# Block 1's attention in 32-token chunks, q rows issued by POOL, memory rows of v loaded once per batch

## The chip, the cores and the metric

The kernel runs on one core of one Trainium2 chip. Times are device microseconds of one execution; a comparison uses the median of several executions. The engines are TensorE (PE, with its weight loads as PEld), VectorE (DVE), ScalarE (ACT), GpSimd (POOL) and SyncE (SP). DMAs are issued from SP's queue, which the profile calls hardware_dynamic, and from POOL's, software_dynamic.

## The reference

Chunked attention with memory rows, then two feed-forward layers with different gates. In float32:

```python
# q, k, v: (4, 8, 768, 64); mem_k, mem_v: (4, 8, 8, 64); chunk 32, 16 keys to the left, 8 to the right
for c in range(768 // 32):
    l_start, r_end = max(0, 32*c - 16), min(768, 32*c + 32 + 8)
    k_full = concat([mem_k, k[:, :, l_start:r_end]]); v_full = concat([mem_v, v[:, :, l_start:r_end]])
    a = softmax(q_c @ k_full.T / 8)
    out[:, :, chunk c] = a @ v_full
x = out as (3072 tokens, 512)
h = x @ moe_w_in; x = (h * tanh(softplus(h))) @ moe_w_out       # 512 -> 2048 -> 512
h = x @ moe2_w_in; x = (h * sigmoid(1.702 * h)) @ moe2_w_out
```

The weights come as float64 and are turned into float32 on the chip.

## The kernel before

**Tiling and stages.** The 3072 tokens are cut into 8 blocks of 384 (TB), two to a batch. `quads` makes the attention of one block after the other, `forward` the first product of layer 1 (16 column tiles f of w_in, 128 columns each). Block 0's `forward` takes float32 matmuls (4 per f, each recorded as two instructions); from block 1 on weights and inputs are split into a high and a low part and three products are summed (12 per f). In the page's lines `forward` is L1218. After block 7's `forward` come the other three products (`across`, `first`, `second`), which the change doesn't touch.

**Two forms of attention.** The rows form (`rows_of_heads`, `turned`, `quad`) serves blocks 0 and 1. It loads rows of q, k and v with 64 channels (256 bytes) of all heads for two groups of 96 queries at a time, 120 keys and 8 memory rows to a group; PE turns q and k (L761), the copies out of PSUM are L768 (ACT) or L769 (DVE); scores are L829 in block 0 and L789 in block 1; VectorE masks and takes the row extremes (L845), ScalarE takes the exponentials (L860), VectorE normalises (L880); PE turns the result (L911 or L991) and multiplies it with v (L928 or L1013). Block 0 goes by `quad_out`, block 1 by `oct_scores` and `oct_out`, which do four groups in one go. The chunk form (`pair_of_heads`, `values_of`, `duo`) serves blocks 2 to 7. It works on 32 queries against 64 keys (16 + 32 + 8 and 8 memory keys). q and k come in pieces of 32 channels (128 bytes) and are turned by VectorE (L669, L672); the memory keys are turned once per batch (`memory_keys`, L632) and copied behind each chunk's keys (L676). A `duo` covers two pairs of heads, so a block has two: scores L1054, VectorE's extremes L1069, exponentials L1076, normalisation L1088, PE's turn L1096, values L1116, then the two parts of x (L1128 or L1130, and L1132).

**Loads.** Rows of blocks 0 and 1, q and k of the later ones, and all weights are issued by SP, one queue in order; block 0's rows may be issued by POOL too (`early`), whichever the planner finds free sooner. v of blocks 2 to 7 is issued by POOL (`via`), 6 loads to a `values_of` (per pair of heads two runs of v and one of mem_v), 12 to a duo.

**Order.** Every step is an `add` with a rank, the engines it may run on with an assumed cost, and what it reads and writes. `Plan.issue` simulates the engines with these costs and hands out, at each moment, the ready step of lowest rank on each engine; that order is the program's order on that engine, and nothing is reordered on the chip. A load is ready when its buffer is free; its assumed transfer time is `bus(bytes, run)`. Ranks count column tiles: `forward(j, f)` has rank 16 j + f. Block 0's attention starts at rank -20, block 1's at -4, block j's at 16 (j-1) - 12 from block 2 on; the loads stand 4 to 8 ahead. The w_in tiles of layer 1 are loaded at rank f - 4.5 (`w_first`), turned into float32 at f - 1.5 (L416 or L419, L425, L429, L433) and split at f + 6 (`w_cut`, L529, L534).

**Buffers.** `T` holds named buffers. In block 0 and 1 the chunk buffers don't exist; at block 2 `more` takes five weight buffers (wo11 to wo15) and `Spread` lays q, k, their turned forms and v (`vh`, four places, two to a duo) over them, z0, z1, z3 and two more `vt`.

Of the kernel before, what the change touches and what calls it, by code (L numbers as in the profile page):

```python
# [9 lines left out]
F32 = mybir.dt.float32  # L10
# [8 lines left out]
EARLY = 2  # L19
WARM = 16  # L20
LEAD = 8
# [5 lines left out]
STAGGER = 1.5  # L27
# [272 lines left out]
def bus(nbytes, run):  # L300
    return nbytes / 290e3 * (1 if run >= 512 else 1.3 if run >= 256 else 1.8)
# [3 lines left out]
def kernel(  # L305
# [64 lines left out]
    def load(rank, buf, parts, nbytes, run, reads=(), early=False, via=None):  # L370

        for part in parts:
            def go(queue, part=part):
                o, i = part()
                queue.dma_start(out=o, in_=i)  # L375

            size = bus(nbytes / len(parts), run)
            ways = [
                ("sp", 0.475, lambda go=go: go(nc.sync), size),
                ("pool", 1.2, lambda go=go: go(nc.gpsimd), size),  # L380
            ]
            add(rank, [("pool", 0.8, *ways[1][2:])] if via else ways if early else ways[:1], reads=reads, writes=[buf])
# [254 lines left out]
    def pair_of_heads(j, hp, rank):  # L637
# [29 lines left out]
        load(rank - 4, ql, qs, P * TB * 4, 128)  # L667
# [20 lines left out]
    def values_of(j, h0, rank):  # L688
# [4 lines left out]
        for i in range(2):  # L693
# [8 lines left out]
            for row, n, r0, c, many in runs:  # L702
# [28 lines left out]
    def rows_of_heads(j, gp, rank):  # L731

        b, s0 = divmod(j * TB, S)
        n = NF - 4 + 2 * j + gp
        qs, ks, vt = (T[nm].new([P, 2, H, D], F32) for nm in (f"wi{n}", f"wo{n}", "vt"))
# [11 lines left out]
        load(rank - 4, ks, kp, size, 256, early=j == 0)  # L747
        load(rank - 4, qs, qp, size * GQ // P, 256, early=j == 0)
        load(rank - 2, vt, vp, size, 256, early=j == 0)
        return qs, ks, vt  # L750

    def turned(j, hp, gp, st, rank):
        qs, ks, _ = st
        t = T["h"].new([P, 2 * (GQ + P)], F32)
        name = ("kT", "qT")[(gp if j else hp) % 2] if j == 0 or hp % 2 else "u"
# [21 lines left out]
    def oct_scores(pairs, rank, names):  # L777

        reads, writes = [x for pair in pairs for p in pair for x in p[2]], []
        cost = 1.4 + 1.0 * (len(pairs) - 1)  # L780
        out = [[T[n].new([GQ, GB, P], F32) for n in ns] for ns in names]

        def scores():
            for pair, s in zip(pairs, out):
                for queries, keys, _ in pair:
                    for i in range(2):
# [24 lines left out]
    def quad(j, hp, gp, heads, rank, given=None, both=None):  # L811
# [64 lines left out]
        if not both:  # L876
            inverses(rank, sm, r)
# [845 lines left out]
```

## Time and profile before

| | us |
|---|---|
| median of 3 runs | 1104.11 |
| lowest and highest run | 1103.93, 1105.63 |
| the profiled execution | 1105.13 |
| its span, first to last instruction | 1103.3 |
| PE, DVE, ACT, POOL busy | 1079.3, 800.3, 555.8, 98.6 |

The profile is of one execution. Busy shares are averages over stages with different limits, so the page is read together with the busy times by stage, the timelines of single engines and the list of waits. A wait is put down to what came last. The ends of matmuls are modelled; the step from one start to the next is the safer measure of what a matmul takes.

### The profile page before, as it was taken

To read this page: it belongs to the slowest core of one execution; us is meant where nothing else is said; L and a number is where in the kernel's file an instruction comes from. 1 tells how busy PE (TensorE), PEld (TensorE's weight loads), DVE (VectorE), ACT (ScalarE), POOL (GpSimd) and SP (SyncE) were. 2 spreads that over 40 slices of the span, in tenths; PEclk is the share of its full clock that TensorE was granted. 3 is DMA by queue.
4 is the path that set the end of the run, shared out by engine and by line. 5 is a ranking of instruction groups with operands and counts; after the bars stand their busy time and mean duration, and the time that the engine had idled before them with its cause. 6 is when DMAs were issued, how large, how long until landed. Compare 5 with 4: busy or idle time off the path is not lost.

```text
span 1103.3 us, 24808 instructions
## 1 busy us (share of the span) xinstructions
PE 1079.3 (98%) x9642; PEld 1041.1 (94%) x9642; DVE 800.3 (73%) x1456; ACT 555.8 (50%) x1246; POOL 98.6 (9%) x169
## 2 busy tenths in 40 slices
PE   7899999999999999999999999999999999999998
PEld 6568898989999999999999999999999999999998
DVE  5997656756556688899879856666657787877875
ACT  5875453545454455555455565555555533333332
POOL 2005642432300000000000000000000000000000
PEclk9999999999999999999999999999999999999999
DMA  9988998899986854663552686868688536345361
GB/s 172 264 241 189 242 247 228 205 250 268 278 276 222 249 175 147 216 212 121 189 172 86 208 260 223 296 227 290 203 265 261 160 106 166 112 133 145 105 165 46
DMA packets 278733, 221.28 MB, mean 201 GB/s; under 512 B 113553, under 2 KB 253868, under 8 KB 278616
## 3 DMA queue, kind: packets, MB, share of 16 engines
q1 hardware_dynamic: 272055, 209.46, 64.9%
q0 software_dynamic: 6560, 10.24, 3.8%
q8 instruction: 76, 1.25, 0.5%
q14 instruction: 42, 0.34, 0.1%
HBM read 138.33 MB, written 81.26 MB: 199 GB/s over the span
## 4 chain that ended last, share of the span: by engine, by line
PE 78%; DMA 10%; DVE 5%; SPq 4%; issue 1%; ACT 1%; DVEq 0%; ACTq 0%
PE o L1481 9%; PE o L1573 9%; PE h L1218 9%; PE o L1218 8%; PE h L1380 7%; PE o L1380 6%; PE s L1481 6%; PE h L1573 6%; PE h L1481 6%; PE s L1573 5%; SPq L375 4%; PE s L1380 3%; DMA st<-wd 3%; DMA st<-in_moe_w_out_dram 2%; DMA g1d<-ev 1%
## 5 line engine op out<-in xcount | busy, mean ns | idle before, releaser
L1218 PE MATMUL h<-xh,wi 128*128 128x384 f32 x320 | 82.9, 340 | 0.0
L1218 PE MATMUL o<-xh,wi 128*128 128x384 f32 x320 | 82.7, 339 | 0.0
L1218 PEld LDWEIGHTS h<-xh,wi 128*128 128x128 f32 x320 | 57.2, 188 | 0.6
L1218 PEld LDWEIGHTS o<-xh,wi 128*128 128x128 f32 x320 | 57.0, 188 | 0.5
L1218 PE MATMUL h<-xl,wi 128*128 128x384 f32 x160 | 53.7, 336 | 0.0
L1218 PE MATMUL o<-xl,wi 128*128 128x384 f32 x160 | 53.7, 336 | 0.0
L1350 ACT ACTIVATE e<-h 128x384 f32<-128x384 f32 (+2 forms) x47 | 22.4, 477 | 45.4 <-PE h L1573 28.8
L1573 PE MATMUL o<-wo,xh 128*128 128x256 f32 x232 | 43.7, 282 | 0.0
L1563 DVE TENSOR_TENSOR xl<-vt,xh 128x1024 fp32r<-128x1024 f32 x24 | 29.3, 1223 | 19.7 <-ACT xh L1560 18.0
L1563 DVE TENSOR_TENSOR xl<-wi,xh 128x1024 fp32r<-128x1024 f32 x32 | 38.8, 1222 | 5.9 <-ACT xh L1560 5.1
L1481 PE MATMUL o<-xh,wo 128*128 128x256 f32 x224 | 40.5, 282 | 0.0
L1560 ACT ACTIVATE xh<-wi 128x1024 fp32r<-128x1024 f32 x25 | 26.4, 1056 | 23.0 <-DMA wi<-gd 12.4
L375 POOL DMA_DIRECT2D vt<-in_v_dram x50 | 32.2, 648 | 63.3 <-PE o L1116 33.6
L375 POOL DMA_DIRECT2D wo<-in_v_dram x50 | 31.7, 638 | 53.7 <-PE o L1116 51.1
L1464 DVE TENSOR_TENSOR xl<-z,xh 128x1024 fp32r<-128x1024 f32 x24 | 29.2, 1222 | 9.7 <-ACT xh L1460 9.1
L1218 PE MATMUL o<-wo,wi 128*128 128x384 f32 x192 | 36.2, 340 | 0.0
L1573 PEld LDWEIGHTS o<-wo,xh 128*128 128x128 f32 x232 | 36.0, 190 | 0.0
L1218 PE MATMUL h<-wo,wi 128*128 128x384 f32 x192 | 35.7, 339 | 0.0
L1481 PEld LDWEIGHTS o<-xh,wo 128*128 128x128 f32 x224 | 34.6, 190 | 0.0
L1218 PEld LDWEIGHTS h<-wo,wi 128*128 128x128 f32 x192 | 33.2, 188 | 0.2
L1218 PEld LDWEIGHTS o<-wo,wi 128*128 128x128 f32 x192 | 33.0, 188 | 0.4
L1350 ACT ACTIVATE ev<-o 128x384 f32<-128x384 f32 (+2 forms) x31 | 14.5, 469 | 36.7 <-PE o L1573 17.5
(460 smaller groups left out, 3499.6 us busy)
## 6 DMA issues: line engine op xcount, KB each, us to landing
st<-in_moe_w_out_dram SPq DMA_DIRECT2D x32, 512.0 KB
st<-wd SPq DMA_DIRECT2D x29, 512.0 KB
z<-g1d SPq DMA_DIRECT2D x24, 512.0 KB
vt<-gd SPq DMA_DIRECT2D x24, 512.0 KB
wi<-gd SPq DMA_DIRECT2D x24, 512.0 KB
g1d<-gl SPq DMA_DIRECT2D x46, 192.0 KB
g1d<-z SPq DMA_DIRECT2D x45, 192.0 KB
wi<-in_moe_w_in_dram SPq DMA_DIRECT2D x16, 512.0 KB
```

The source lines that it names most:

```text
L375: queue.dma_start(out=o, in_=i)
L1218: nc.tensor.matmul(out=h.get(), lhsT=a[:, c], rhs=b.at(kk), start=(n == 0), stop=(n == KD * len(prods) - 1))
L1350: ("act", act(n, True), lambda: nc.scalar.activation(out=dst(), in_=bank.get(), func=AF.Copy)),
L1380: nc.tensor.matmul(out=bank.get(), lhsT=a, rhs=b, start=(fresh and m == 0), stop=(m == 3 * K2 - 1), skip_group_check=not fresh,)
L1464: add(rank + 0.05, [("dve", dve(n2), lambda gh=gh, gl=gl, src=src: nc.vector.tensor_tensor(out=flat(gl), in0=flat(src), in1=flat(gh), op=A ...
L1481: nc.tensor.matmul(out=bank[:, d, :], lhsT=a, rhs=b[:, p, :], start=(fresh and h == d == p == m == 0), stop=(h == 1 and p == HP - 1 and m ...
L1560: ("act", act(NP * P), lambda: nc.scalar.activation(out=flat(gh), in_=flat(src), func=AF.Copy)),
L1563: add(rank + 0.05, [("dve", dve(NP * P), lambda: nc.vector.tensor_tensor(out=flat(gl), in0=flat(src), in1=flat(gh), op=ALU.subtract))], re ...
L1573: nc.tensor.matmul(out=bank.get(), lhsT=a[:, p], rhs=b, start=(fresh and p == 0 and m == 0), stop=(p == NP - 1 and m == 2), skip_group_che ...
```

## The change

Block 1 goes through the chunk form (`pair_of_heads`, `values_of`, `duo`) instead of the rows form. `EARLY`, `LEAD`, `STAGGER`, `oct_scores`, `oct_out` and the arguments that served them go. The chunk buffers are laid out at block 1, in another order of places: the first duo's q, k and v go to wo11 to wo15 and only later ones to z0, z1 and the two `vt`. Block 0's staging buffers move from wo12 and wo13 to wo8 and wo9. `memory_keys` is called for the first batch too, at rank -9. q from block 2 on is issued by POOL (`via=NARROW * (j > 1)`); a load from POOL has an assumed cost of 0.64 instead of 0.8. `values_of` loads the memory rows of v only in the first block of a batch and in block 1; in blocks 3, 5 and 7 the four `vh` places still hold them. `bus` assumes other transfer times: longer ones for short rows from SP, shorter ones from POOL. All of block j + 1's attention is handed to the planner before `forward(j, 0)`, in block 1 too.

```diff
-EARLY = 2
-LEAD = 8
-STAGGER = 1.5
+NARROW = 0.64
...
-def bus(nbytes, run):
-    return nbytes / 290e3 * (1 if run >= 512 else 1.3 if run >= 256 else 1.8)
+def bus(nbytes, run, soft=False):
+    if soft:
+        return nbytes / 290e3 * (1.07 if run >= 256 else 1.45)
+    return nbytes / 290e3 * (1 if run >= 512 else 1.75 if run >= 256 else 1.93)
...
-    def load(rank, buf, parts, nbytes, run, reads=(), early=False, via=None):
+    def load(rank, buf, parts, nbytes, run, reads=(), via=0, either=False):
...
-            size = bus(nbytes / len(parts), run)
-            ways = [
-                ("sp", 0.475, lambda go=go: go(nc.sync), size),
-                ("pool", 1.2, lambda go=go: go(nc.gpsimd), size),
-            ]
-            add(rank, [("pool", 0.8, *ways[1][2:])] if via else ways if early else ways[:1], reads=reads, writes=[buf])
+            way = ("sp", 0.475, lambda go=go: go(nc.sync), bus(nbytes / len(parts), run))
+            if via:
+                way = ("pool", via, lambda go=go: go(nc.gpsimd), bus(nbytes / len(parts), run, True))
+            ways = [way]
+            if either:
+                ways.append(("pool", 1.2, lambda go=go: go(nc.gpsimd), bus(nbytes / len(parts), run, True)))
+            add(rank, ways, reads=reads, writes=[buf])
...
-        load(rank - 4, ql, qs, P * TB * 4, 128)
+        load(rank - 4, ql, qs, P * TB * 4, 128, via=NARROW * (j > 1))
...
-            parts.append(lambda row=i * D + CHUNK, h=h: (
-                vt[row:row + NM], rows(mem_v, h * NM, [(1, NM), (0, NCH)], 0, D)
-            ))
-        load(rank, vt, parts, P * NCH * D * 4, 256, via="pool")
+            if s0 == 0 or j == 1:
+                parts.append(lambda row=i * D + CHUNK, h=h: (
+                    vt[row:row + NM], rows(mem_v, h * NM, [(1, NM), (0, NCH)], 0, D)
+                ))
+        load(rank, vt, parts, P * NCH * D * 4, 256, via=NARROW)
...
-        n = NF - 4 + 2 * j + gp
-        qs, ks, vt = (T[nm].new([P, 2, H, D], F32) for nm in (f"wi{n}", f"wo{n}", "vt"))
+        n = NF - 4 + gp
+        qs, ks, vt = (T[nm].new([P, 2, H, D], F32) for nm in (f"wi{n}", f"wo{n - 4}", "vt"))
...
-    def oct_scores(pairs, rank, names):
...
-    def oct_out(j, rank, vt, heads):
...
-            if j == EARLY:
+            if j == 1:
...
-                T["ql"] = Spread(pre, (z0, 0), (more[3], 0))
-                T["kl"] = Spread(pre, (z0, TB), (more[3], TB))
-                T["qT"] = Spread(pre, *((z, 0) for z in (z1, *more[:2])))
-                T["kT"] = Spread(pre, *((z, 448) for z in (z1, *more[:2])))
+                T["ql"] = Spread(pre, (more[3], 0), (z0, 0))
+                T["kl"] = Spread(pre, (more[3], TB), (z0, TB))
+                T["qT"] = Spread(pre, *((z, 0) for z in (*more[:2], z1)))
+                T["kT"] = Spread(pre, *((z, 448) for z in (*more[:2], z1)))
...
-                T["vh"] = Spread(pre, *((z, 0) for z in (*vs, more[2], more[4])))
+                T["vh"] = Spread(pre, *((z, 0) for z in (more[2], more[4], *vs)))
...
-            base = NF * (j - 1) - (4 if j < EARLY else SOON)
-            if s0 == 0 and j + 1 >= EARLY:
-                memory_keys(b, base)
+            base = NF * (j - 1) - (4 if j < 2 else SOON)
+            if s0 == 0:
+                memory_keys(b, base + (11 if j == 0 else 0))
...
-                attention(j + 1, (f + LEAD) // 2 if j + 1 < EARLY else NQ)
+                attention(j + 1, NQ)
```

## Rows read from the trace of the kernel before

**Rows 1.** The page: busy time, the chain that ended last, POOL's queue.
```profile
PE 1079.3 (98%) x9642; PEld 1041.1 (94%) x9642; DVE 800.3 (73%) x1456; ACT 555.8 (50%) x1246; POOL 98.6 (9%) x169
...
q0 software_dynamic: 6560, 10.24, 3.8%
...
PE 78%; DMA 10%; DVE 5%; SPq 4%; issue 1%; ACT 1%; DVEq 0%; ACTq 0%
```

**Rows 2.** Windows by stage: start:end length, busy us of each engine, PE clock, DMA share, GB/s.
```profile
0.00:39.07 39.07, 28.50 (x272) 23.67 (x272) 24.79 (x134) 24.71 (x99) 5.94 (x14) 0.96 1.01 201
39.07:94.21 55.14, 53.79 (x371) 33.41 (x369) 51.60 (x150) 39.52 (x124) 3.58 (x7) 1.00 0.88 230
94.21:141.38 47.17, 45.42 (x788) 42.92 (x787) 30.05 (x84) 23.68 (x104) 33.55 (x56) 1.00 0.95 232
141.38:182.78 41.40, 41.10 (x590) 39.44 (x590) 24.63 (x66) 19.04 (x77) 16.22 (x27) 1.00 0.88 232
182.78:225.59 42.81, 41.30 (x590) 39.37 (x589) 28.99 (x72) 20.84 (x72) 15.17 (x26) 1.00 0.84 221
...
345.62:379.20 33.58, 33.58 (x194) 33.57 (x194) 20.68 (x35) 17.27 (x31) 0.00 (x0) 1.00 0.79 239
379.20:1103.30 724.10, 717.38 (x5378) 714.40 (x5376) 548.87 (x740) 352.79 (x561) 0.00 (x0) 1.00 0.58 181
```

**Rows 3.** Windows of the same columns from 25 to 75 us.
```profile
25.00:50.00 25.00, 20.81 (x161) 14.04 (x162) 23.64 (x94) 23.04 (x87) 0.00 (x0) 1.00 0.98 242
50.00:75.00 25.00, 23.80 (x141) 14.88 (x140) 24.23 (x63) 16.44 (x46) 0.80 (x2) 1.00 1.03 298
```

**Rows 4.** Windows of the same columns, rows of 256 and of 128 bytes.
```profile
15.00:20.00 5.00, 2.80 (x20) 2.55 (x20) 1.41 (x9) 1.94 (x7) 0.00 (x0) 0.76 1.00 178
...
80.00:85.00 5.00, 5.00 (x30) 2.96 (x29) 5.00 (x14) 3.53 (x16) 0.00 (x0) 1.00 0.60 98
```

**Rows 5.** PE's timeline in the prologue: start, us, what, [idle before <-releaser].
```profile
17.20 0.27 PE L761 MATMUL h<-ident,wi 96*128 96x96 f32 x1 [3.48 <-DMA wi<-in_q_dram]
...
38.59 0.55 PE L928 MATMUL o<-z,vt 128*64 128x96 f32 x8 [1.16 <-DVE z L918]
```

**Rows 6.** VectorE's timeline in the prologue.
```profile
20.45 0.29 DVE L845 CUSTOM_DVE_ANT_0 e<-s,mask 96x128 f32<-96x128 f32 x1 [4.04 <-PE s L829]
20.66 0.08 DVE L845 DVE_READ_ACCUMULATOR2_ANT mx<- 96x1 f32 x1
...
21.63 0.61 DVE L769 COPY z<-h 128x448 f32<-128x448 f32 x1
...
31.03 0.43 DVE L419 TENSOR_SCALAR wo<-wi 128x512 f32<-128x512 f32 x1 [1.20 <-DMA wi<-in_moe_w_in_dram]
```

**Rows 7.** PE's timeline in block 0's forward.
```profile
45.40 5.35 PE L1218 MATMUL o<-xh,wo 128*128 128x384 f32 x16
50.59 0.25 PE L761 MATMUL h<-ident,wi 96*128 96x96 f32 x1
...
89.91 0.24 PE L1054 MATMUL s<-z 64*32 64x64 f32 x1
...
91.01 0.88 PE L1013 MATMUL o<-z,vt 128*64 128x96 f32 x16
```

**Rows 8.** Who waited for w_in's tiles, us and times.
```profile
  ACT wo L416: 4.1, 4
```

**Rows 9.** PE's waits from 94.2 to 310 us: total, times, longest.
```profile
PE s L1096 <- DVE e L1088: 1.5, 1, 1.5
PE s L1054 <- issue: 1.3, 2, 1.0
...
PE o L1054 <- issue: 0.7, 1, 0.7
```

**Rows 10.** POOL's loads of v: ns min/median/max, first and last start.
```profile
L375 POOL DMA_DIRECT2D vt<-in_v_dram x50: 574/645/964, 2.7 to 267.9; - x50
...
DMA to landing us min/median/max: 2.7/4.7/7.9
```

More of the change, by code (lines that the diff above doesn't have):

```diff
@@ L746, in rows_of_heads @@
         size = P * 2 * H * D * 4
-        load(rank - 4, ks, kp, size, 256, early=j == 0)
-        load(rank - 4, qs, qp, size * GQ // P, 256, early=j == 0)
-        load(rank - 2, vt, vp, size, 256, early=j == 0)
+        load(rank - 4, ks, kp, size, 256, either=True)
+        load(rank - 4, qs, qp, size * GQ // P, 256, either=True)
+        load(rank - 2, vt, vp, size, 256, either=True)
         return qs, ks, vt
@@ L775, in turned @@
         )
-    def oct_scores(pairs, rank, names):
[L779 to L786, printed above, removed]
-                        for hh in range(2):
-                            d = slice(hh * D, (hh + 1) * D)
-                            nc.tensor.matmul(
-                                out=s[hh][:, keys(d, i, True), :],
-                                lhsT=queries(d, i), rhs=keys(d, i), start=True, stop=True,
-                            )
-        add(
-            rank + 0.5, [("pe", cost, scores)],
-            reads=list(dict.fromkeys(reads)), writes=writes + [x for s in out for x in s],
-        )
-        return out
     def inverses(rank, sm, r):
@@ L809, in inverses, with quad @@
         add(rank + 1.4, [("dve", 0.16, inverse)], updates=[r])
-    def quad(j, hp, gp, heads, rank, given=None, both=None):
+    def quad(j, hp, gp, heads, rank):
         b, s0 = divmod(j * TB, S)
@@ L814, in quad @@
         queries, keys, turned_from = heads
-        first = 2 * gp if given else 0
         names = (("s0", "s1"), ("o0", "o1"))[hp % 2]
-        after = names if j else ("o2", "o3")
-        s = given or [T[n].new([GQ, 2, P], F32) for n in names]
-        e = T["ev" if j != 1 and hp % 2 else "e"].new([GQ, 2, 2, P], F32)
+        s = [T[n].new([GQ, 2, P], F32) for n in names]
+        e = T["ev" if hp % 2 else "e"].new([GQ, 2, 2, P], F32)
         mx = T["mx"].new([GQ, 2, 2], F32)
-        sm, r = both or [T[n].new([GQ, 2, 2], F32) for n in ("sm", "r")]
+        sm, r = [T[n].new([GQ, 2, 2], F32) for n in ("sm", "r")]
         done = fixed()
@@ L835, in scores @@
                     )
-        if given:
-            after = (names[gp],) * 2
-        else:
-            add(rank + 0.5, [("pe", 0.87, scores)], reads=turned_from, writes=s)
+        add(rank + 0.5, [("pe", 0.87, scores)], reads=turned_from, writes=s)
         def least(hh):
@@ L874, in quad @@
                 )
-        if not both:
-            inverses(rank, sm, r)
+        inverses(rank, sm, r)
         def norm():
@@ L881, in norm @@
                 out=e.get(), in0=e.get(), op=ALU.mult,
-                in1=r[:, first:first + 2].unsqueeze(3).to_broadcast([GQ, 2, 2, P]),
+                in1=r.get().unsqueeze(3).to_broadcast([GQ, 2, 2, P]),
             )
@@ L888, in norm_act @@
                     nc.scalar.activation(
[L889 removed]
+                        out=e[:, i, hh, :], in_=e[:, i, hh, :], func=AF.Copy, scale=r[:, i, hh:hh + 1]
                     )
[L892 to L898 removed]
+        add(rank + 1.4, [("dve", dve(4 * P), norm), ("act", 4 * act(P), norm_act)], reads=[r, done], updates=[e])
+        return ("o2", "o3"), e
     def quad_out(j, hp, gp, vt, rank, names, e):
@@ L921, in quad_out @@
         )
[L923 removed]
+        g, h = 0, 2 * hp
         def values():
```

90 lines of the change are left out of this document (7 added, 83 removed).

## The prediction

> **What bounds the kernel now.** I read the page first, then the windows by stage, then TensorE's timeline. The page has PE busy 98% of the span and 78% of the chain that ended last [rows 1]: the kernel is a queue of matmuls, and a change pays if it takes time out of that queue where it is full. The windows are cut where the forward matmuls (L1218) of a block begin. The first stage, block 0's attention, has PE busy 28.50 of 39.07 us. From 39.07 on PE is full: 53.79 of 55.14 us for block 0, and 717.38 of 724.10 us after 379.2 [rows 2]. What moves a block boundary therefore moves the end by as much; behind 379.2 there is no idle stretch to swallow it.
>
> Two more resources are nearly full in the front. VectorE is busy 23.64 and 24.23 of 25 us from 25 to 75 us, and the DMA engines have shares of 0.98 and 1.03 there [rows 3]; from 15 to 20 us the share is 1.00 too [rows 4]. Block 0's prologue shows who waits for them: PE waits 3.48 us for q rows of the second half, and its last values 1.16 us for a VectorE copy [rows 5]; VectorE starts on that half at 20.45 after 4.04 us idle and later waits 1.20 us for the first w_in tile [rows 6].
>
> **Block 1 in chunk form, the matmul side.** Block 0's forward has 128 matmuls. Sixteen of them take 50.59 - 45.40 = 5.19 us, so 0.324 each and 41.5 in all; the scores of block 2's first duo take 91.01 - 89.91 = 1.1 [rows 7]. What is left of the 55.14 us is 12.5: the turned, score, transpose and value matmuls of block 1, with 1.35 us idle. The cost of the new form is read where only it runs. A block of forward alone takes 33.58 us (the stage from 345.62; 33.4 without a stray matmul of the next phase), and the stage from 141.38 holds the same forward with the scores, transposes and values of two duos: 41.40 - 33.4 = 8.0, idle 0.3 included; the next stage gives 42.81 - 33.4 = 9.4 with 1.5 idle [rows 2]. So block 1 in chunk form costs 8.0 and, if the old 1.35 us idle stays, 9.35 in place of 12.5: -3.15. The first duo's scores (1.1) carry rank -2.5, ahead of the first forward matmul, and need only the PSUM that block 0's last score reduction gives back. I place them before 39.07, where PE has room: -4.25. The bounds are -3.15 - 0 (nothing fits ahead, and 1.4 more idle as in the second stage: -1.75) and -5.6 (all idle goes too).
>
> **The prologue.** Two things pull apart. (1) The old form put its k and q rows, 1.84 MB in rows of 256 bytes, ahead of the first w_in tile. At the 178 GB/s that such rows get at a full share [rows 4] that is 10.3 us. The new first duo puts 0.82 MB in rows of 128 bytes there. At 98 GB/s with a share of 0.60, thus 163 at a full one [rows 4], it is 5.0 us. w_in comes some 5 us earlier, so the 1.20 us wait of VectorE goes, and block 1's old reductions and evictions in this stage (8 reductions x 0.21, from one start to the next, + 2 evictions x 0.61 = 2.9 us [rows 6]) give way to four transposes and a reduction of the new one, about as much. (2) The v rows of that first duo are 12 loads on POOL, and their buffers (wo12, wo14) are free from the start. Nothing holds them back: POOL, whose last work before 39 us is over early (5.94 us of it in all, none from 15 to 20) [rows 2, 4], issues them as soon as its share of block 0's loads is out (near 7 us, an estimate from those 5.94), and so past SP's queue, in which block 0's second half still stands. 0.79 MB at POOL's rate (10.24 MB in 3.8% of the span, 244 GB/s [rows 1]) is 3.2 us, at 178 GB/s 4.4 us, and PE and VectorE were already waiting for that second half [rows 5, 6]. Bounds for the start of the forward: 3.5 us earlier (the 1.2, and 2.3 if most of the new ones wait until after 39) to 4.4 later. I take 0: the gain of (1) is paid for (2).
>
> **The rest of the front.** The whole of block 1 needs 2.88 MB at 178 GB/s = 16.2 us of DMA before and 2 x (5.0 + 3.2) = 16.4 after, so the w_in stream is as late at its end as before. But PE would ask for each tile earlier, and ScalarE already waited 4.1 us in four pieces for w_in [rows 8]. I charge 0.5 (0 to 4.1). Matmuls in chunk form are many and tiny (198 for a duo, so 396 for block 1, against 192 in the old form), and in three of the places that hold them PE waits for nothing the profile names ("issue", 1.3 and 0.7 us in two lines of the stretch from 94 to 310 [rows 9]): 2.0 us for the ten duos there, 0.2 each, 0.4 for two more; I charge 0.4.
>
> **q by POOL, memory rows once.** From block 2 on 96 loads of 48 KB leave SP, whose queue is 4% of the chain [rows 1], and go to POOL, where a load takes 0.645 us [rows 10]. Memory rows fall away in blocks 3, 5 and 7: 24 loads. A block then asks POOL for 16 + 24 loads, 25.8 us of some 42, or 20.6 without the memory rows. Behind a q load stand the v loads of the next duo, which are used some 20 us later; behind a v load that waits for its buffer stands q, which is read one duo later. Both have more slack than 12 x 0.645 = 7.7 us. The DMA time of q goes from 163 GB/s (4.7 MB, 29 us over six blocks) to anything up to 244 (19 us), since no POOL load of 128-byte rows is in the trace; the memory rows save 0.59 MB, 2.4 us. PE waits for no such load in these stages; its waits there are for VectorE's normalisation (1.5 us) and issue [rows 9]. So I take 0 with bounds -2 and +2. VectorE's work falls by little and ScalarE's by about half of block 1's, both hidden behind PE.
>
> **The sum.** -4.25 + 0 + 0.5 + 0.4 + 0 = -3.35 against the profiled execution, 1105.13 us (span 1103.3 and 1.8 around it). That execution lies 1.0 above the median of the runs, 1104.11, so the forecast for the runs is 1104.11 - 3.35 = 1100.8.
>
> **A rule against it.** POOL's issues took 0.645 us in the median and 0.96 at most, and the data landed 4.7 us later in the median [rows 10], beside a VectorE that was 59 to 68% busy [rows 2]; in the front it is 95% busy [rows 3]. If VectorE held POOL up there, block 1's 24 v loads would take longer: issued one behind another from 25 us, they reach past the end of block 0's forward, near 90, from (90 - 25) / 24 = 2.7 us each. The Trainium skill, "SBUF — State Buffer", section "SBUF: two separate sides", says just that: a VectorE instruction in a two-port mode locks GpSimd out of the port through which it writes descriptors, and such a DMA of about 620 ns took about 3100. By that rule the last values would come near 100. The trace bears none of it out at 59 to 68%: no issue is longer than 0.96 us [rows 10].
>
> **The rivals.** (B) The v rows of the first duo don't delay block 0's second half, because POOL's queue only fills gaps: the forward starts up to 3.5 us earlier, 1097.3. For it: PE's and VectorE's waits in the prologue are single ones [rows 5, 6]. Against: the DMA share is already 1.00. (C) The front is set by VectorE and w_in, not by PE: VectorE has 51.60 us of work in the 55.14 of block 0's forward [rows 2], and its new transposes, reductions and normalisations stand in for as many old ones. If it sets the pace the stage shrinks by no more than its idle 3.5 us; I take half, 1.5 to 2 in place of 4.25: 1102.5 to 1104.5. For it: 95% busy from 25 to 75. Against: PE waited for it for 1.35 us only. (D) Slower: the loads of the first duo, v by POOL and q and k behind, all get ahead of block 0's second half. That is 3.2 + 5.0 = 8.2 us on q rows that PE already waits for; less the 2.4 of other work saved in the prologue the forward starts 5.8 later, and with -4.25 + 0.9 behind it the end is +2.4: 1106.5, up to 1109. It decides from the point at which those rows land more than 5.8 us after 17.2. For it: POOL doesn't wait for SP. Against: q and k stay on SP behind block 0's. (E) POOL held up by VectorE as above: values near 100, block 1's forward 6 to 9 us late, 1110 to 1113. (F) q by POOL pays in DMA time and the idle between 94 and 310 goes: 2 us better than the forecast, 1098.8; it is inside the range.
>
> **Chances.** Forecast with its own range 1098 to 1102.4, F in it: 0.48. B 0.14, C 0.20, D 0.14, E 0.04. Faster by over 0.2% is below 1101.9, slower is above 1106.3; that is about what a measurement of this kernel can tell from no change. Faster: B and most of the forecast, 0.58; same: C and the forecast's upper edge, 0.23; slower: D and E, 0.19. The range goes from 1096.0 to 1106.5 and leaves out E, the half of D beyond 2.4, and the lowest of B.
>
> **What would show it.** Right: L789, L991, L1013 gone from block 1; the stage from the first forward of block 0 to that of block 1 near 51 us; its start within 2 us of 39; a wait of PE or VectorE for block 0's second q rows that is longer than 3.5 us, with POOL's v loads issued before 15 us; block 1's stage and those after it as long as before; POOL's q issues near 0.65 us. Wrong: a stage of 53 us or more with PE waiting for L433 or L534 (C); a start at 36 (B) or past 43 (D); POOL issues of 2 us and more (E); or PE's waits between 94 and 310 changed by more than 2 us, for then the order of the later blocks, which I take as unchanged, has moved the time.

## The result, and the profile after

The changed kernel takes 1115.14 us in the median of 4 runs against 1104.87 for the kernel before beside it: a ratio of 1.0086, 95% interval 1.006 to 1.0112. It is 10 us slower; the forecast was 1100.8, 3.3 faster, and the range ended at 1106.5. In the profiled execution (1114.69, span 1112.9) the stages, cut as in [rows 2], are these (start:end and length, busy us of PE, PEld, DVE, ACT, POOL, then PE's granted clock as a share of 2.4 GHz, DMA share, GB/s); the line from 141.38 is the kernel before, for blocks 2 to 5:

```profile
0.00:41.64 41.64, 28.63 (x225) 23.15 (x225) 25.27 (x123) 22.32 (x85) 17.35 (x33) 0.78 0.98 177
41.64:106.38 64.74, 55.49 (x623) 33.67 (x621) 49.74 (x117) 32.27 (x113) 27.76 (x48) 0.88 0.93 218
106.38:152.42 46.04, 45.35 (x789) 43.14 (x788) 30.21 (x86) 22.19 (x92) 33.32 (x56) 1.00 0.88 218
152.42:316.59 164.17, 163.91 (x2354) 158.14 (x2353) 107.83 (x281) 74.95 (x278) 81.35 (x133) 1.00 0.91 255
386.04:1112.90 726.86, 719.10 (x5379) 716.52 (x5377) 549.08 (x739) 351.99 (x560) 0.00 (x0) 1.00 0.58 180
```

```profile
141.38:309.84 168.46, 164.81 (x2354) 157.73 (x2354) 103.23 (x269) 81.42 (x298) 55.49 (x93) 1.00 0.93 250
```

Against [rows 2] the forward starts 2.6 us later, block 0's stage is 9.6 longer, block 1's 1.1 shorter, blocks 2 to 5 are 4.3 shorter, and the part from 379 on is 2.8 longer; together the 9.6 of the spans. The last part is the same work, and in the profiled executions of all kernels below it lies between 723 and 728, so its 2.8 is no effect of the change. The loss stands in block 0's stage: PE idle 9.25 us (64.74 - 55.49) in place of 1.35, at a clock of 0.88 in place of 1.00.

PE's timeline of the changed kernel shows the four places (start, us, line, [idle before <-releaser]):

```profile
19.98 0.39 PE L763 MATMUL h<-ident,wi 96*128 96x96 f32 x1 [5.03 <-DMA wi<-in_q_dram]
41.64 8.14 PE L1110 MATMUL h<-xh,wo 128*128 128x384 f32 x16
49.62 2.75 PE L1110 MATMUL o<-xh,wo 128*128 128x384 f32 x8
88.25 0.87 PE L1002 MATMUL s<-ident,e 128*128 128x128 f32 x3 [6.15 <-DVE e L994]
91.17 1.65 PE L1110 MATMUL h<-xh,wo 128*128 128x384 f32 x2 [2.04 <-ACT z L1242]
```

The wait for q rows is 5.03 and ends at 19.98 (3.48 and 17.20 before [rows 5]). The first 16 forward matmuls take 7.98 from one start to the next group's, against 5.19 at full clock [rows 7]. And 40 us into the stage PE waits 6.15 us for the normalisation of block 1's second duo, then 2.04 for a copy of ScalarE. What stood behind the 6.15 is read on ScalarE and VectorE:

```profile
78.87 0.15 DVE L977 TENSOR_SCALAR mx<-mx 128x6 f32<-128x6 f32 x1
79.20 0.67 ACT L417 ACTIVATE wo<-wi 128x512 f32<-128x512 f32 x1 [3.49 <-DMA wi<-in_moe_w_in_dram]
82.84 0.66 ACT L417 ACTIVATE wo<-wi 128x512 f32<-128x512 f32 x1 [2.97 <-DMA wi<-in_moe_w_in_dram]
83.40 0.30 ACT L982 ACTIVATE e<-s,mx 128x64 f32<-128x64 f32 x1
87.56 0.55 DVE L994 TENSOR_TENSOR e<-e,r 128x384 f32<-128x384 f32 x1
```

The row maximum that the exponentials (L982) need is there at 79.0. They begin at 83.40: ahead of them in ScalarE's fixed order stand two casts of w_in tiles that had not landed. All its waits for w_in in the front make 13.4 us (4.1 before [rows 8]). The tiles are late on SP's queue (SPq: the time in which SP issues a group of loads):

```profile
29.04 4.32 SPq L375 DMA_DIRECT2D wi<-in_moe_w_in_dram  x6
33.41 2.03 SPq L375 DMA_DIRECT2D st<-in_moe_w_out_dram  x2
35.54 8.83 SPq L375 DMA_DIRECT2D z<-in_q_dram  x4
44.42 6.37 SPq L375 DMA_DIRECT2D z<-in_k_dram  x4
52.88 1.02 SPq L375 DMA_DIRECT2D wi<-in_moe_w_in_dram  x2
72.41 1.24 SPq L375 DMA_DIRECT2D wi<-in_moe_w_in_dram  x2
```

w_in's tiles 0, 6 and 12 are issued at 29.04, 52.88 and 72.41. In the kernel before it was earlier each time:

```profile
25.50 4.25 SPq L375 DMA_DIRECT2D wi<-in_moe_w_in_dram  x5
47.26 2.04 SPq L375 DMA_DIRECT2D wi<-in_moe_w_in_dram  x4
64.72 1.03 SPq L375 DMA_DIRECT2D wi<-in_moe_w_in_dram  x2
```

Block 1's q and k rows of 128 bytes hold SP for 8.83 and 6.37 us, because what was issued just ahead of them, 3 MB of w_in and 1 MB of w_out, has to pass first and then the q rows themselves; the DMA engines are full then (first line, same columns as the windows above). Where only such rows are under way the engines are not full:

```profile
35.00:50.00 15.00, 12.85 (x54) 7.93 (x55) 13.11 (x28) 9.58 (x26) 5.33 (x10) 0.66 1.08 248
25.00:30.00 5.00, 5.00 (x35) 4.00 (x34) 3.89 (x22) 3.14 (x13) 0.00 (x0) 0.50 0.41 66
26.00:27.00 1.00, 1.00 (x8) 0.72 (x7) 0.74 (x7) 0.75 (x4) 0.00 (x0) 0.50 0.06 4
28.00:30.00 2.00, 2.00 (x15) 1.50 (x15) 1.44 (x8) 0.76 (x4) 0.00 (x0) 0.50 0.62 101
50.00:55.00 5.00, 5.00 (x32) 2.74 (x38) 3.04 (x6) 1.34 (x4) 0.00 (x0) 1.00 0.60 103
51.00:54.00 3.00, 3.00 (x11) 1.81 (x10) 2.04 (x4) 0.49 (x1) 0.00 (x0) 1.00 0.63 103
```

From 28 to 30 and from 51 to 54 us all packets are under 512 bytes: 101 and 103 GB/s at shares of 0.62 and 0.63, with POOL issuing nothing. That is the pace at which SP issues, four loads of 48 KB in 1.95 us, thus 101 GB/s:

```profile
50.89 1.95 SPq L375 DMA_DIRECT2D wo<-in_q_dram  x4
```

The 66 GB/s hold a gap as well: near 26 us SP issues nothing and waits 1.8 us for rows of v to land. The same queue can do more with such rows. In the kernel before, q and k loads of the same kind were issued while w_out still passed, and when their turn came they ran at a full share; from 44 to 45 us all packets there are under 512 bytes too:

```profile
39.10 0.83 SPq L375 DMA_DIRECT2D st<-in_moe_w_out_dram  x2
40.04 2.01 SPq L375 DMA_DIRECT2D wo<-in_q_dram  x4
42.09 2.97 SPq L375 DMA_DIRECT2D wo<-in_k_dram  x4
...
44.00:45.00 1.00, 1.00 (x4) 0.52 (x3) 1.00 (x6) 1.00 (x5) 0.00 (x0) 1.00 1.07 166
```

### The profile page after: what moved, and what is told of

It reads as the page before. It is cut to its first block, busy times and chain, and to the rows that moved or that the text cites. A ratio compares the mean times of both kernels' runs of the same rounds, so it can differ in the third digit from the quotient of the medians.

```text
span 1112.9 us, 25192 instructions
## 1 busy us (share of the span) xinstructions
PE 1081.9 (97%) x9846; PEld 1043.7 (94%) x9846; DVE 803.9 (72%) x1424; ACT 536.8 (48%) x1195; POOL 159.8 (14%) x269
## 4 chain that ended last, share of the span: by engine, by line
PE 87%; DMA 6%; SPq 3%; DVE 2%; issue 1%; POOL 1%; ACT 0%; DVEq 0%; ACTq 0%
PE h L1110 11%; PE o L1110 11%; PE o L1465 9%; PE o L1373 9%; PE h L1272 8%; PE o L1272 7%; PE h L1465 6%; PE h L1373 6%; PE s L1465 6%; PE s L1373 6%; PE s L1272 4%; SPq L375 3%; PE s L1022 1%; DMA wo<-in_v_dram 1%; DMA st<-wd 1%
## 5 line engine op out<-in xcount | busy, mean ns | idle before, releaser
L1110 PE MATMUL h<-xl,wi 128*128 128x384 f32 x160 | 53.8, 336 | 0.0
L1110 PE MATMUL o<-xl,wi 128*128 128x384 f32 x160 | 53.8, 336 | 0.0
L1242 ACT ACTIVATE e<-h 128x384 f32<-128x384 f32 (+2 forms) x47 | 22.4, 476 | 46.9 <-PE h L1465 28.7
L375 POOL DMA_DIRECT2D vt<-in_v_dram x60 | 38.6, 650 | 40.5 <-PE o L1022 20.8
L375 POOL DMA_DIRECT2D wo<-in_v_dram x56 | 35.6, 642 | 38.2 <-PE o L1022 29.8
L1373 PE MATMUL o<-xh,wo 128*128 128x256 f32 x224 | 40.5, 282 | 0.0
L1242 ACT ACTIVATE ev<-o 128x384 f32<-128x384 f32 (+2 forms) x32 | 15.1, 471 | 41.2 <-PE o L1465 17.1
L982 ACT ACTIVATE e<-s,mx 128x64 f32<-128x64 f32 x84 | 25.0, 316 | 19.3 <-DVE mx L977 19.3
```

The lines of the kernel that those rows point to most:

```text
L982: nc.scalar.activation(out=e[:, g, i], in_=s[hh][:, g, i], func=AF.Exp, scale=scale, bias=mx[:, g, i:i + 1], accum_out=sm[:, g, i:i + 1],)
L1110: nc.tensor.matmul(out=h.get(), lhsT=a[:, c], rhs=b.at(kk), start=(n == 0), stop=(n == KD * len(prods) - 1))
L1242: ("act", act(n, True), lambda: nc.scalar.activation(out=dst(), in_=bank.get(), func=AF.Copy)),
L1373: nc.tensor.matmul(out=bank[:, d, :], lhsT=a, rhs=b[:, p, :], start=(fresh and h == d == p == m == 0), stop=(h == 1 and p == HP - 1 and m ...
```

## The experiments

The theory after the result: block 1's rows of 128 bytes block SP's one queue, w_in comes late behind them, ScalarE stands in order at the late tiles, and PE waits and loses its clock. Rivals: the order or the figures of the planner; v taken too early; too many bytes in that stretch, in whatever queue; the clock by itself. All stages are of the profiled execution; "start" and "stage" are the first forward matmul of block 0 and the time from there to that of block 1; times are medians beside the kernel before on the same chip (1103.5 to 1104.6).

### Each part alone

The chunk form for block 1 with all of q left to SP and the memory rows in every block:

```diff
-        load(rank - 4, ql, qs, P * TB * 4, 128, via=NARROW * (j > 1))
+        load(rank - 4, ql, qs, P * TB * 4, 128, via=0)
-            if s0 == 0 or j == 1:
+            if True:
```

> The changed kernel with q issued by SP throughout and the memory rows of v loaded in every block: the chunk form for block 1 and the new transfer times alone. If the two small parts only help (5 us in blocks 1 to 5), this is 3 to 6 us slower than the changed kernel, 1118 to 1121, with the same idle stretch of PE near 82 us. If q on POOL is part of what delays the front, it is faster than the changed kernel, 1105 to 1112, and block 0's stage is shorter than 64.7 us.

1125.88, ratio 1.0202 (1.0167 to 1.0238): slower than the changed kernel, by more than the 3 to 6 us of the first case. Block 0's stage is 61.9, and now blocks 2 and 3 suffer too: 46.1 and 46.8 in place of 41.4 and 42.8 [rows 2].

The other two parts in the kernel before, together and one at a time, and the planner's new figures alone (`bus` and 0.64 as in the change's diff):

```diff
-        load(rank - 4, ql, qs, P * TB * 4, 128)
+        load(rank - 4, ql, qs, P * TB * 4, 128, via=0.64)
...
+            if s0 == 0:
```

> The kernel before, block 1 in the rows form, with only two parts of the change: q from block 2 on by POOL (assumed cost of a POOL load 0.64), memory rows of v once per batch; the assumed transfer times as before. If the 5 us that blocks 1 to 5 got shorter in the changed kernel come from these two parts, this one is 3 to 5 us faster than before (1100 to 1102) and its first block boundary stays near 94 us. If they come from the new order that block 1's chunk form and the new transfer times give, it is within 1 us of before. If q on POOL is what delays w_in, block 0's stage is longer than 55 us.

> The kernel before, with the memory rows of v loaded once per batch and nothing else. Theory M (the gain of blocks 2 to 5 comes from DMA time and POOL issues saved by the memory rows): blocks 2 to 5 together 3 us shorter than the 168.4 of the kernel before. Theory Q (it comes from q leaving SP's queue): blocks 2 to 5 within 1 us of it, time within 1104 +- 2. Of the 5.8 us wait in the middle of block 1's score matmuls that the run with both showed: if the memory rows bring it, it shows here too.

> The kernel before, with q from block 2 on issued by POOL at 0.64 and nothing else. Theory Q: blocks 2 to 5 together 3 to 4 us shorter than the 168.4 of the kernel before, and the time 1100 to 1102 if no wait of 5.8 us shows in block 1's stage, 1106 if it does. Theory M: blocks 2 to 5 as long as before or longer, since POOL gets 96 loads more without losing the 24 of the memory rows; 1104 to 1107.

> The kernel before with the planner's new figures alone (the time it reckons for a transfer by row length and by queue, and 0.64 for an issue by POOL): the same instructions and bytes, in the order that the new figures give. Theory: the figures are not what costs; every stage is within 1 us of the kernel before, 1103 to 1106. Rival: the figures bring a worse order of their own, block 0's stage 57 or more, 1107 or more.

| | time | ratio (95%) | block 0 | block 1 | blocks 2 to 5 |
|---|---|---|---|---|---|
| before | | | 55.1 | 47.2 | 168.5 |
| both | 1106.76 | 1.0022 (1.0005, 1.0040) | 55.3 | 52.5 | 164.3 |
| memory rows | 1101.31 | 0.9978 (0.9963, 0.9992) | 54.8 | 45.5 | 167.3 |
| q by POOL | 1105.30 | 1.0028 (1.0007, 1.0049) | 54.3 | 49.8 | 166.9 |
| figures | 1106.86 | 1.0037 (1.0016, 1.0057) | 56.2 | 49.6 | 165.5 |

None of them touches block 0's stage by more than 1.1 us: the loss there belongs to the chunk form with its loads. The memory rows alone are a gain, and that kernel is faster than both. Blocks 2 to 5 shrink towards some 164 in several ways, even by the figures alone; 164 is their PE work without waits (163.91 busy above), so this gain has no single owner; theories M and Q asked 3 us and more of one part, and each gave 1.2 and 1.5. The figures alone bring a worse order in blocks 0 and 1 and a better one behind, and cost 3 us in all: between their two theories. With q by POOL block 1's stage grows by a wait that names no releaser, in the middle of a score burst (here of the run with both):

```profile
PE s L1055 <- issue: 5.8, 1, 5.8
```

All five such waits above 1 us in these kernels and the one before (5.78, 3.76, 1.89, 1.82, 1.05) lay where 96 value matmuls and 96 score matmuls touched. So one run, with q by POOL and the memory rows once, kept the two apart:

```diff
+                    if e == "pe" and dense and held is None and op.ways[w][1] in (COSTS, COSTV):
+                        held = item
+                        continue
```

> The kernel before with q from block 2 on by POOL and the memory rows once per batch (the second run of the first batch), and one rule more in the planner: on TensorE a duo's 96 value matmuls and the next duo's 96 score matmuls never stand back to back, a piece of the forward goes between. Theory P (TensorE runs dry of instructions when two such bursts touch: all four waits above 0.7 us that name no releaser lie in such a pair): the wait of 5.8 us and the fall of the clock behind it go, block 1's stage falls from 52.5 to 44 to 47, and the time is 1097 to 1100, faster than the kernel before. Rival L (what fails is the instruction load itself, late beside the data transfers of that moment): the wait moves to the next burst, 3 to 6 us, and the time is 1104 to 1107.

1105.70, ratio 1.0029 (1.0004 to 1.0053): the wait is 2.6 us and stands in a burst by itself. Theory P falls; that PE's instructions came late is not shown either, and this wait stays open. (The profiled execution took 1101.40, the least of the ten, so its stages don't show what the median has beyond that.)

### What block 0's stage waits for

Three edits of the changed kernel, and the first two together: v behind block 0's second half, w_in ranked earlier, the planner told of the late tiles.

```diff
-                T["vh"] = Spread(pre, *((z, 0) for z in (more[2], more[4], *vs)))
+                T["vh"] = Spread(pre, *((z, 0) for z in (*vs, more[2], more[4])))
...
-            load(rank - 3, st, [lambda: (
+            load(rank - 3 - (6 if layer == 1 else 0), st, [lambda: (
...
-            )], P * 8 * DM, 1024, pace_by)
+            )], P * 8 * DM, 1024, pace_by, late=(11,) if layer == 1 and f > 11 else ())
```

> The changed kernel with the four places of v in the old order: the first duo of block 1 gets the two vt buffers, which block 0 holds until its value matmuls, so POOL cannot issue its v loads before about 30 us. If these loads, issued from 6.7 us on, are what makes block 0's second q rows land at 19.98 instead of 17.20 us, PE's wait for them is back near 3.5 us, the first forward matmul starts 2 to 3 us earlier (39 us), and the time falls by 2 to 3 us or, if the low clock from 36.9 to 47.1 us goes with it, by 5 to 6: about 1109 to 1112. If the late stretch from 82 to 95 us is a consequence of the prologue too, it falls by 10 or more. If the v loads are innocent (theory of the w_in queue alone), the start stays at 41 to 42 us and the time at 1115.

> The changed kernel with layer 1's w_in loads ranked 6 column tiles earlier, so that SP issues them ahead of the q and k loads of block 1 and 2. If late w_in tiles are the cause (casts on ScalarE wait for them, the exponentials of block 1's second duo queue behind the casts, PE idles 6.1 us at 82 us and its clock is halved for 10.2 us), the wait of PE for the normalised scores goes, the granted clock stays at 1.00 from 50 us on, and the time falls by 8 to 12 us to 1103 to 1107. If block 1's chunk form is slow by itself (VectorE and ScalarE the bound of block 0's stage), the stage from the first forward to block 1's stays above 60 us and the time near 1115. If the rows of q and k now come too late, PE waits for the scores instead: 1110 to 1120.

> The changed kernel with both edits of the two runs before it: the first duo's v rows take their buffers behind block 0's second half, and w_in's loads are ranked six steps earlier. Theory S (two causes in different places, the prologue's q rows and the late w_in tiles in block 0's stage): the gains add, the forward starts near 40 as with the first edit alone, block 0's stage is 57 to 60 us as with the second alone, no wait of TensorE in it is above 3 us, and the time is 1103 to 1106. Rival T (one and the same shortage of DMA time, paid in whichever place is behind): the second edit adds little to the first, block 0's stage stays at 61 us or the start goes back to 43, and the time is 1108 to 1110.

> The changed kernel; the planner alone is told that the w_in tiles 12 to 15 land 11 us later than it reckons, about as late as the trace shows them; no load, byte or instruction is added or taken away. It then puts the second duo's exponentials ahead of the casts of tiles 12 and 13 on ScalarE. Theory S (ScalarE stands in order at a cast whose tile is late, and the exponentials behind it are what TensorE waits for): the exponentials start near 79 in place of 83.4, the wait of 6.15 us for the normalisation and the fall of the clock behind it go, block 0's stage falls from 64.7 to 57 to 60, and the time is 1107 to 1110. Rival W (the tiles themselves set the pace, the exponentials only stand where the wait shows): TensorE waits as long for the splits of tiles 12 and 13 instead, the stage stays at 63 or more, and the time is 1114 to 1116.

To compare them I take PE's busy time in the stage less length x (1 - clock), its work at full clock; where PE waits within the slow stretch this is too small.

| | time | ratio (95%) | start | stage | PE idle | clock | work at full clock | ACT waits for w_in |
|---|---|---|---|---|---|---|---|---|
| before | | | 39.1 | 55.1 | 1.4 | 1.00 | 53.8 | 4.1 |
| changed | 1115.14 | 1.0086 (1.0060, 1.0112) | 41.6 | 64.7 | 9.3 | 0.88 | 47.7 | 13.4 |
| v behind | 1109.74 | 1.0050 (1.0033, 1.0068) | 39.8 | 61.5 | 5.9 | 0.93 | 51.3 | 14.8 |
| w_in earlier | 1109.58 | 1.0041 (1.0022, 1.0060) | 43.5 | 59.4 | 5.4 | 0.95 | 51.0 | 10.4 |
| both | 1108.09 | 1.0046 (1.0029, 1.0062) | 40.9 | 60.3 | 5.5 | 0.93 | 50.6 | 11.2 |
| told late | 1112.20 | 1.0076 (1.0056, 1.0097) | 40.5 | 63.0 | 7.4 | 0.85 | 46.2 | 5.3 |

With v behind the rows PE waits 1.44 us for them in place of 5.03, the forward starts 1.8 earlier, and the time is in the expected 1109 to 1112:

```profile
16.57 0.27 PE L763 MATMUL h<-ident,wi 96*128 96x96 f32 x1 [1.44 <-DMA wi<-in_q_dram]
```

So v's early loads did delay block 0's second half. With w_in earlier the time came out between the cases, 1109.58, and the forward started 1.8 later: other loads of the queue now came late. The two gains do not add (theory S falls, T comes nearer), and telling the planner, which does take the exponentials from behind the casts, shortens the stage by under 2: rival W by the stage, though the time lies between the two cases. The order on ScalarE was where most of the lateness showed, not what made it. What the transfers bring too late, some step waits for.

### The clock

Three matmuls of the identity ahead of the values of block 0's last four quads, in the changed kernel and in the one with both edits:

```diff
+        def fill():
+            for _ in range(3):
+                nc.tensor.matmul(out=o[:, 0], lhsT=ident.get(), rhs=ident[:, :GQ], start=True, stop=True)
+        if gp:
+            add(rank + 2.3, [("pe", 0.75, fill)], reads=[ident, t], writes=[o])
```

> The changed kernel with three matmuls of 96 columns, of the identity by itself, between the transposes and the values of each of the four last quads of block 0; they overwrite nothing that is read. Theory K (the old form's scores kept TensorE busy in block 0's prologue; with them gone it works in snatches, and the clock is at half when the forward starts): the granted clock is full at the first forward matmul, the first 16 take 5.2 us in place of 7.98, and the time falls by 2 to 3, to 1112 to 1113. Rival N (the clock fell for the wait for q rows at 15 to 20 us and comes back by itself as fast with or without work): half clock stays in place as long, and the 0.75 us of each of the four fillings is added: 1115 to 1117.

> The changed kernel with v behind block 0's second half, w_in ranked six steps earlier, and the fillings of the run before. If the three causes (v ahead of the q rows, w_in tiles late for ScalarE, the clock at half at the first forward) are separate, it is 2 to 3 us below the 1108.1 that the first two give: 1105 to 1106; the fall of the clock from 29 to 46 us is gone. If the clock is a consequence of the waits that are left, it stays at 1108.

Windows of the first (prologue, block 0), and PE's longest wait in the second:

```profile
0.00:40.00 40.00, 30.07 (x249) 24.96 (x249) 25.12 (x122) 22.02 (x85) 17.32 (x33) 0.87 1.00 185
40.00:101.40 61.40, 53.87 (x623) 32.31 (x621) 49.53 (x119) 33.85 (x115) 29.43 (x49) 0.94 0.94 234
```

```profile
PE s L1008 <- DVE r L782: 8.1, 1, 8.1
```

The first gives 1110.45, ratio 1.0069 (1.0044 to 1.0094), with a higher clock in both stretches (0.87 and 0.94 for 0.78 and 0.88), the way theory K has it, though not yet full at the start: the first 16 forward matmuls take 6.0 us (39.99 to 46.02), 0.5 of it a wait, for K's 5.2. The interval overlaps that of the changed kernel. The second gives 1113.36, ratio 1.0099 (1.0069 to 1.0129): the planner's order is another one again, and PE waits 8.1 us for a step of a normalisation. The lower clock costs time in the profile, yet no run isolates how much.

### The queue

Now the transfers themselves. q by POOL from block 1 on, with the same bytes; the same with v behind; w_out's two loads held back; all three:

```diff
-        load(rank - 4, ql, qs, P * TB * 4, 128, via=NARROW * (j > 1))
+        load(rank - 4, ql, qs, P * TB * 4, 128, via=NARROW * (j > 0))
...
-        pace_by = begun[-1 - AHEAD:-AHEAD] if (layer, part) == (1, 0) else []
+        pace_by = begun[-1 - AHEAD:-AHEAD] if layer == 1 else []
```

> The changed kernel with q issued by POOL from block 1 on, in place of block 2. Theory H (SP's queue is held by block 1's q rows, 8.83 us for one head pair, and w_in stands behind them): w_in's tile 6 is issued near 45 in place of 52.9, tile 12 near 65 in place of 72.4, the wait of 6.15 us shrinks below 2, block 0's stage falls to 57 to 59, and the time to 1106 to 1109. Rival B (the bytes of the stretch are too many, in whichever queue): tiles 12 and 13 land as late as before, the stage stays at 62 or more, and the time is 1112 to 1116.

> The same, and v of the first duo takes its buffers behind block 0's second half. Theory H with the prologue as a separate cause: the forward starts at 39 to 40, block 0's stage is 57 to 59, and the time 1103 to 1106. Rival B: start 39 to 40, stage 61 or more, 1108 to 1111.

> The changed kernel with the two loads of w_out, 0.5 MB each, which SP issues at 33.4 ahead of block 1's q rows, held back until w_in's conversion has come nearer; nothing else. Rival B: 1 MB less is 3.6 to 4.6 us of transfers, the w_in tiles come by so much earlier, block 0's stage falls by 3 to 5 us, and the time is 1110 to 1112. Theory H: SP's queue is held as long behind those rows, tile 6 comes no more than 2 us earlier, and the stage is shorter by less than 2.

> All three edits: q by POOL from block 1 on, v behind block 0's second half, w_out held back. If the transfers of that stretch were what was left, no wait of TensorE above 2 us remains between 40 and 100 us, the stage is 52 to 56 and the time 1098 to 1102, faster than the kernel before. If something else sets the pace (VectorE's conversions, the clock), the stage stays at 58 or more and the time is 1104 to 1108.

| | time | ratio (95%) | start | stage | PE idle | clock | work at full clock | ACT waits for w_in |
|---|---|---|---|---|---|---|---|---|
| q from block 1 | 1103.63 | 0.9994 (0.9972, 1.0016) | 43.3 | 52.9 | 1.1 | 0.97 | 50.3 | none listed |
| and v behind | 1107.95 | 1.0029 (1.0006, 1.0051) | 39.9 | 57.3 | 2.2 | 0.92 | 50.6 | 9.1 |
| w_out held | 1108.36 | 1.0035 (1.0017, 1.0053) | 40.4 | 61.8 | 5.5 | 0.91 | 50.7 | 7.7 |
| all three | 1106.79 | 1.0026 (1.0003, 1.0049) | 40.0 | 60.1 | 5.5 | 0.92 | 49.8 | 9.1 |

One comparison in one line takes the loss away: with q by POOL from block 1 on, the ratio falls from 1.0086 to 0.9994, the intervals apart. Its stages, two windows, and SP's queue:

```profile
0.00:43.30 43.30, 30.68 (x225) 24.44 (x225) 25.55 (x123) 23.27 (x86) 24.82 (x45) 0.72 1.05 206
43.30:96.20 52.90, 51.84 (x623) 32.29 (x621) 48.41 (x115) 31.58 (x113) 30.72 (x49) 0.97 0.99 232
...
45.00:50.00 5.00, 5.00 (x15) 2.80 (x15) 5.00 (x10) 1.53 (x3) 3.06 (x5) 0.90 1.17 219
50.00:55.00 5.00, 5.00 (x17) 2.71 (x15) 4.70 (x10) 2.06 (x4) 3.60 (x5) 1.00 1.23 211
```

```profile
26.50 4.40 SPq L375 DMA_DIRECT2D wi<-in_moe_w_in_dram  x6
30.95 1.96 SPq L375 DMA_DIRECT2D st<-in_moe_w_out_dram  x2
32.95 8.12 SPq L375 DMA_DIRECT2D z<-in_k_dram  x4
41.11 4.45 SPq L375 DMA_DIRECT2D wi<-in_moe_w_in_dram  x2
```

Tile 6 of w_in is issued at 41.11 in place of 52.88: 2.5 of these 11.8 us stand at tile 0 already (26.50 for 29.04), and SP no longer spends 8.83 and 1.95 on q loads ahead of it. The DMA share from 50 to 55 us is 1.23 in place of 0.60, with w_in's tiles among the loads, and PE has no wait above 0.7 us in the stage. Theory H holds, and by more than it said (a stage of 52.9 for 57 to 59). Rival B of these runs, the bytes, is not the whole: they are the same. But 1 MB less ahead of the rows helps as well, and by more than theory H allowed: with w_out held tile 6 goes out at 46.30, 6.6 earlier, and the stage is 3.0 shorter. Both fit the one queue, with less in front or with less to carry. With each such edit the planner's order on the engines changes somewhat too, so how much of the 10 us is the order's is not separated. With v behind as well the forward starts 3.4 earlier, and block 1's still begins no earlier (97.2 against 96.2): in that pair the prologue's loss was not on what sets the end of the stage. The stage came out as theory H said, the time did not: 1107.95 for 1103 to 1106. All three together came out by the second case, 60.1 and 1106.79. Tile 12 of w_in goes out at 52.34 there, 12 us earlier than in the kernel before, yet ScalarE waits 9.1 us for w_in and 7.0 for the forward's results on their way out (`g1d`), which SP issues as well. So q on POOL alone does not settle every order of the rest, and what holds these two kernels is open.

Two last runs, on the version with q from block 1 on: with the fillings, and with block 1's k by POOL too.

```diff
-        load(rank - 4, kl, ks, P * NKB * 128, 128)
+        load(rank - 4, kl, ks, P * NKB * 128, 128, via=NARROW * (j == 1))
```

> q by POOL from block 1 on, and the three matmuls of the identity ahead of the values of block 0's last four quads. That version's forward began at 43.3 with the clock at half from 18.7 to 46. If the thin work of TensorE is what keeps the clock down, the fillings bring the full clock back before the first forward matmul, the forward starts near 40 and the time is 1097 to 1101, faster than the kernel before. If the late start comes from the transfers (q of block 1 beside q of block 0's second half) and the clock follows, start and clock stay and it is 1103 to 1105.

> The same, with block 1's k rows by POOL too. If SP's queue is still held by k's rows of 128 bytes (8.12 and 3.65 us in the version with q alone), tiles 6 to 15 of w_in land another 3 to 6 us earlier; block 0's stage, which has no wait above 0.7 us left, can gain at most 2 us, and the time is 1096 to 1101. If POOL then holds the first scores back (28 issues of 0.65 for a duo, 18 us), TensorE waits for kT of the second duo and the stage grows by 3 or more: 1104 to 1108.

The first: 1101.66, ratio 0.9990 (0.9968 to 1.0013), start 43.9, stage 52.3, idle 0.6: as far as can be told no faster than the kernel before. The fillings didn't bring the start forward, which the expectation laid to the transfers. The second: 1109.35, ratio 1.0058 (1.0034 to 1.0081). Start 45.8, stage 55.3, with 1.6 us behind a copy that POOL makes itself:

```profile
PE s L966 <- POOL wo L677: 1.6, 1, 1.6
```

ScalarE's waits for w_in are 4.7 there (5.4 in the first). The stage is 3.0 longer than in the first, as the expectation's second case has it; that POOL's queue is now the one that is too full rests on this one wait and is not shown further, and the profiled execution took 1105.21, the least of the twelve.

## Why the prediction was wrong

**The step that failed** is (1) in "The prologue": the new first duo's 0.82 MB in rows of 128 bytes, "at 98 GB/s with a share of 0.60, thus 163 at a full one", were to pass in 5.0 us ahead of w_in, so that "w_in comes some 5 us earlier". The first w_in tile was issued 3.5 us later (29.04 for 25.50), although only eight of those 16 loads stood ahead of it. The other eight stood behind six tiles of w_in and w_out, held SP for 8.83 and 6.37 us, and tile 6 behind them was 5.6 later. The row was right; the scaling to a full share holds only for loads that have piled up in the queue (166 GB/s at 1.07 in the kernel before). Rows that went alone got SP's pace, 101 to 103 GB/s, which makes 8 us of the 0.82 MB (0.82 / 0.101) and leaves a good third of the DMA engines' time idle, and beside v from POOL they were later still. Everything behind them in the queue waits. The same slip stands in "The rest of the front", where 16.2 us of DMA before and 16.4 after made w_in "as late at its end as before"; its tile 12 was issued 7.7 us later, and the 0.5 that I charged (bound 4.1) became 13.4 us of ScalarE's waits, 9.25 us of PE idle for 1.35, and a clock of 0.88. With q's rows on POOL the loss was gone (0.9994).

**Block 1's matmuls** were right. By lines, the old form's matmuls in block 0's stage make 11.3 us (3.55 + 1.96 + 3.52 + 2.23), the new ones 8.05 (L960 3.68 less a third, which is block 2's, L1002 2.40, L1022 3.20): -3.2 for -3.15. In the tables the work at full clock is 49.8 to 51.3 in the kernels whose slow stretches don't fall into waits, 2.5 to 4 below the 53.8 of before, and near the 51 of the forecast's stage. But the first duo's scores (-1.1) did not come ahead of the forward: they started at 54.9, since half of their rows stood in that queue until 50.8.

**The prologue**, taken as 0 in a range of -3.5 to 4.4, came out at +2.6 by the mechanism of (2) and of rival D: POOL issued v from 6.66 us on, and PE's wait rose to 5.03; with v behind it was 1.44. D's own point, q rows more than 5.8 us after 17.2, was not reached (2.8). What I left out is the clock: 272 matmuls ran in the old prologue at 0.96 [rows 2], 225 in the new at 0.78, and the forward began at half speed.

**Rival C** named w_in, but as a pace that VectorE sets; VectorE was 77% busy (49.74 of 64.74), and PE waited for L994 and L1242, not for the conversions. A late tile in front of other work in an in-order engine cost waits, 9.25 us idle for 1.35, and not a slower pace.

**q by POOL and the memory rows** were taken as 0 within 2. Blocks 1 to 5 came out 5.4 shorter (rival F's gain, and more than its 2), with no single owner, as the runs of the parts show. I argued that PE waits for no such load from block 2 on. With block 1 in chunk form that did not hold: with q on SP throughout and the memory rows in every block, blocks 2 and 3 lost 4.7 and 4.0 us, and VectorE waited 4.5 us there for q rows. From that kernel over the changed one to q by POOL from block 1 on the ratios are 1.0202, 1.0086 and 0.9994; the first of these steps takes out the memory rows as well. **Rival B** fell too: in no version of the changed kernel did the forward begin near 36.

**Rival E** fell: POOL's 19 loads from 25 to 75 us took 582 to 644 ns a group beside the busy VectorE, as in [rows 10]:

```profile
L375 POOL DMA_DIRECT2D vt<-in_v_dram x8 | 5.1, 642 | 19.7 <-PE o L897 19.7
L375 POOL DMA_DIRECT2D wo<-in_v_dram x4 | 2.6, 644 | 14.4 <-PE o L1022 14.4
```

With q on POOL too, the slowest group of its loads there took 742 ns on average, far from E's 2.7 us. The Trainium skill's rule of the lock ("SBUF — State Buffer", "SBUF: two separate sides") is borne out by no load of POOL here: the longest single issue of any run took 1.1 us.

## What to carry to other kernels

Price short rows by the pace at which one engine issues them, and scale to a full DMA share only where the loads will have piled up in the queue; list what stands ahead of them in that queue and what stands behind. A form that saves matmuls but needs narrower loads should get its loads onto a second queue in the same step; here that one comparison was worth some 10 us, more than three times what the matmuls saved. Where an edit's gain comes back as a wait at another step each time the order is changed, look for the shared resource under the order.

## What the runs showed of the hardware

Loads of 128-byte rows that SP issued with nothing ahead of them kept the DMA engines 0.62 to 0.63 busy at 101 to 103 GB/s, the pace of SP's issues (four loads of 48 KB in 1.95 us). Such loads that had piled up behind w_out in the same queue ran at 166 GB/s and 1.07. SP itself was held when much stood ahead: four such loads took it 8.83 us behind 4 MB of weights. The Trainium skill, "DMA: Bandwidth & Descriptors", section "Issuing engines are not separate DMA queues", says that issuing on several engines saves only the issuer's time, usually small beside the transfer. Here the issuer's time was not small: 0.49 us for 48 KB, which at 166 GB/s pass in 0.30, and 8.83 us for four such loads behind those weights. With the same bytes, taking q's loads off SP was worth 10 us of the kernel.

TensorE stood still in the middle of bursts of 96 to 192 tiny matmuls for 1 to 5.8 us with no releaser, and with the bursts kept apart a wait of 2.6 was left; its cause stays open. After the 5.03 us wait for q rows the granted clock was at the 1.2 GHz level (0.50 from 25 to 30 us), and it was low again when the forward began, at the end of a prologue with 47 matmuls fewer (225 for 272): the first 16 forward matmuls took 7.98 us for 5.19.
